# Attention and two MLP stages on one core: four like PSUM slots in place of two kinds of bank

## The chip, the cores and the metric

The kernel runs on one core of one Trainium2 chip. The metric is the device time of one execution in microseconds (us). Before the change its median is 464.29 us over three runs (463.94 to 465.4).

## What is computed

Causal attention over 2 batches of 12 heads (448 tokens, 64 wide), then two MLP stages on the 896 tokens of 768 values. All in float32.

```python
scores = (q @ k.T) / sqrt(64), causal mask
attn = exp(scores - max); attn = attn / (sum + 1e-9)
x = attn @ v                          # heads side by side: 896 x 768
h = x @ w_in                          # 896 x 1024
solu = h * softmax(h)
x = layernorm(solu) * g_ln @ w_out    # 896 x 768
out = relu(x @ w_in2) ** 2 @ w_out2   # 2048 wide in between
```

## The kernel before

The 24 heads are worked as 12 pairs; a pair's two heads lie on partitions 0 to 63 and 64 to 127. For each pair i the string `SEQ` (line 27) names these steps, and its order is the order of the instructions on every engine, written out by hand; each engine's queue is in order.

- `load_r`, `load_v` (SP queue) fetch keys with queries, and values. `H` (ACT, line 255) rounds keys and queries to float32r, `L` (DVE, line 259; pair 0 on POOL) takes the rest.
- `S0a`, `S0b`, `S0c` (PE, line 270) are rough scores of row blocks 3, 2 with 0, and 1. `mxa`, `mxb`, `mxc` (DVE, line 285) take the maximum of each row. `mT` (PE, line 293) transposes the eight columns of maxima, `row` (ACT, line 298) copies them out of PSUM, and `rowd` (SP, lines 310 and 314) writes them as rows of `MR`. Pair 0 goes another way (`mxr`, line 305).
- `Sa`, `Sb` (PE, lines 329, 337, 345) are the exact scores in two halves, the maximum subtracted by a matmul of `NEG1` with `MR`. `ea1`, `eb1` (ACT, line 361) are their exponentials, `ka`, `kb` (POOL, line 358) the mask.
- `Ua`, `Ub` (PE, line 370) multiply with the values. `EA`, `EB` (ACT, line 382) copy the result of either head out of PSUM. `sums`, `recips`, `rcd`, `spread`, `norm`, `x_hi`, `x_lo` divide by the row sums, by way of three transfers, and leave `xT`.
- `wf`, `wh`, `wl` prepare the weights of the first MLP. `h0.c` to `h6.c` (PE, line 488) are the six matmuls of one token tile with chunk c; the last attention steps are mixed with them. Then come `y` (line 635), the second MLP's `h` (line 769) and `o` (line 798).
- `fl` (line 517) is two matmuls of 448 columns whose result nobody reads: `NEG1` by the zeros in `MR[2]`. There are ten, all ahead of the first exact scores.

PSUM has eight banks of 512 float32 a partition. Before, `bank2` hands out two slots of two banks (exact scores, fills, `h`), and `bank` four single banks (each head's rough scores, each head's U, the transpose). A slot is taken from the head of a list and put back at its end when the step that reads it stands in the order; the wait on that reader is attached to the first instruction that writes the slot. When `EB` of the last pair has been placed, the four single banks become two more slots of two.

```python
bs = [bank("mxp") for h in range(2)]            # max_mm
UB[i] = [bank("U") for h in range(2)]           # pv
nc.scalar.activation(ee[i][:, h, :], U[:, 0:S], AF.Identity, bias=SE)   # EA, EB
nc.tensor.matmul(b[:, j % 2, 0:S], NEG1, MR[2][:, 0:S], start=True, stop=True)  # fl
```

Of the kernel before, what the change touches and what calls it, by code (L numbers as in the profile page):

```python
# [26 lines left out]
SEQ = """
load_r.0 lq.0 fl.0 fl.1 fl.2 H.0 load_r.1 fl.3 lq.8 lq.1 L.0 S0b.0 fl.4 mxb.0 fl.5 S0a.0 fl.6 mxa.0 S0c.0 H.1 load_r.2
fl.7 lq.4 fl.8 mxc.0 load_v.0 S0c.1 fl.9 mxc.1 S0a.1 mxr.0 lq.2 mxa.1 S0b.1 Sa.0 mxb.1 H.2 load_r.3 mT.1 S0a.2 row.1
Sb.0 ea1.0 mxa.2 load_v.1 ka.0 lq.3 lq.5 S0b.2 eb1.0 rowd.1 Ua.0 mxb.2 lq.9 H.3 kb.0 L.1 S0c.2 Ub.0 mxc.2 load_r.4 L.2  # L30
mT.2 Sa.1 row.2 L.3 EA.0 rowd.2 EB.0 S0a.3 ea1.1 Sb.1 lq.6 mxa.3 sums.0 lq.10 S0c.3 ka.1 eb1.1 mxc.3 load_r.5 S0b.3
load_v.2 mxb.3 Sa.2 H.4 kb.1 S0c.4 mT.3 mxc.4 Sb.2 row.3 L.4 rowd.3 S0b.4 Ua.1 recips.0 mxb.4 rcd.0 H.5 load_r.6 ea1.2
wf.0 Ub.1 eb1.2 spread.0 load_v.3 S0a.4 EA.1 Sa.3 EB.1 kb.2 mxa.4 sums.1 S0c.5 Sb.3 ka.2 mxc.5 mT.4 norm.0 S0b.5 row.4
wh.0 mxb.5 Ua.2 rowd.4 ea1.3 recips.1 rcd.1 x_hi.0 ka.3 S0a.5 load_v.4 H.6 Ub.2 mxa.5 eb1.3 wl.0 S0a.6 spread.1 EA.2
Sa.4 load_r.7 EB.2 kb.3 mxa.6 sums.2 mT.5 Sb.4 row.5 x_lo.0 ea1.4 rowd.5 L.5 S0b.6 Ua.3 norm.1 mxb.6 H.7 recips.2
S0c.6 Ub.3 rcd.2 mxc.6 ka.4 eb1.4 load_r.8 x_hi.1 L.6 S0a.7 EA.3 Sa.5 EB.3 kb.4 mxa.7 spread.2 lq.7 mT.6 Sb.5 row.6
L.7 sums.3 ea1.5 rowd.6 S0c.7 x_lo.1 Ua.4 H.8 load_v.5 ka.5 mxc.7 eb1.5 norm.2 S0b.7 recips.3 Ub.4 mxb.7 rcd.3
load_v.6 L.8 S0c.8 load_r.9 EA.4 Sa.6 EB.4 kb.5 mxc.8 spread.3 Sb.6 wf.1 lq.11 sums.4 mT.7 Ua.5 row.7 x_hi.2 rowd.7
ea1.6 H.9 load_r.10 S0b.8 x_lo.2 Ub.5 mxb.8 eb1.6 norm.3 wh.1 recips.4 S0a.8 rcd.4 mxa.8 Sa.7 load_v.7 ka.6 EA.5 EB.5
S0c.9 kb.6 mT.8 mxc.9 Sb.7 sums.5 row.8 x_hi.3 spread.4 wl.1 ea1.7 S0a.9 rowd.8 Ua.6 eb1.7 mxa.9 load_r.11 ka.7 H.10  # L40
x_lo.3 S0b.9 recips.5 Ub.6 norm.4 mxb.9 rcd.5 S0a.10 Sa.8 mxa.10 kb.7 EA.6 spread.5 x_hi.4 mT.9 L.9 S0c.10 EB.6 Sb.8
row.9 sums.6 ea1.8 x_lo.4 Ua.7 rowd.9 mxc.10 H.11 L.10 load_v.8 eb1.8 ld.3 norm.5 S0b.10 recips.6 Ub.7 rcd.6 mxb.10
S0b.11 kb.8 x_hi.5 Sa.9 mxb.11 EA.7 ka.8 EB.7 mT.10 Sb.9 wf.2 sums.7 row.10 ea1.9 rowd.10 S0a.11 Ua.8 eb1.9 spread.6
load_v.9 ka.9 mxa.11 wh.2 Sa.10 recips.7 x_lo.5 rcd.7 S0c.11 Sb.10 mxc.11 norm.6 mT.11 load_v.10 Ub.8 row.11 ea1.10
rowd.11 L.11 x_hi.6 spread.7 Ua.9 EA.8 x_lo.6 eb1.10 kb.9 EB.8 ka.10 Sa.11 sums.8 load_g.0 kb.10 Ub.9 ld.4 norm.7
recips.8 Sb.11 wf.3 Ua.10 EA.9 ea1.11 EB.9 x_hi.7 h0.0 sums.9 eb1.11 load_v.11 wl.2 rcd.8 h0.1 wh.3 kb.11 h1.0 wf.4
spread.8 Ub.10 ld.5 h0.2 wl.3 wh.4 h1.1 recips.9 ka.11 rcd.9 x_lo.7 Ua.11 norm.8 Ub.11 wf.5 EA.10 x_hi.8 h1.2 EB.10
sums.10 h0.3 spread.9 wl.4 wh.5 h1.3 x_lo.8 wl.5 h0.4 norm.9 recips.10 h0.5 rcd.10 h1.4 mx.0 EA.11 h1.5 spread.10
EB.11 ex.0 sums.11 h2.0 x_hi.9 x_lo.9 h2.1 de.0 norm.10 recips.11 mx.1 rcd.11 h2.2 mu.0 h2.3 x_hi.10 spread.11 sq.0
x_lo.10 h3.0 ex.1 va.0 pw.0 h2.4 mu.1 norm.11 h2.5 sq.1 h3.1 mx.2 x_hi.11 h3.2 de.1 ex.2 x_lo.11 va.1 lw.0 h3.3 pw.1  # L50
mu.2 h3.4 fa.1 fa.0 de.2 ln.0 h3.5 sq.2 T.0 mx.3 lw.1 h4.0 va.2 ex.3 of.0 pw.2 h4.1 ln.1 h4.2 Th.0 fa.2 mu.3 oh.0 h4.3
ln.2 lw.2 ol.0 T.1 sq.3 of.1 h4.4 h4.5 de.3 oh.1 Tl.0 h5.0 Th.1 lw.3 mx.4 h5.1 va.3 ex.4 Tl.1 h6.0 pw.3 mu.4 T.2 l2.0
h5.2 de.4 sq.4 fa.3 ol.1 lw.4 h5.3 ln.3 of.2 h5.4 Th.2 T.3 of.3 h5.5 h6.1 mx.5 lw.5 h6.2 Tl.2 ex.5 h6.3 Th.3 de.5 mu.5
h6.4 oh.3 Tl.3 sq.5 h6.5 lw.6 va.4 oh.2 y0.0 mx.6 ol.2 ex.6 ol.3 y0.1 de.6 va.5 mu.6 lw.7 pw.5 l2.1 pw.4 l2.2 fa.4
of.4 ln.4 y0.2 fa.5 oh.4 of.5 y0.3 sq.6 ol.4 oh.5 va.6 ln.5 T.4 ol.5 pw.6 y0.4 Th.4 of.6 Tl.4 oh.6 y0.5 fa.6 ol.6 ln.6
of.7 T.5 y0.6 Th.5 oh.7 Tl.5 ol.7 T.6 y0.7 Th.6 Tl.6 f2.0 y1.0 yo.1 g2.0 f2.1 o2.0 y1.1 yp.0 yo.2 g2.1 yo.0 o2.1 y1.2
yp.1 yp.2
# [3 lines left out]
def attention_moe_kernel(tc, kq, v, w_in, w_out, g_ln, w_in2, w_out2, out):  # L61
# [27 lines left out]
    def f(ap):  # L89
        return ap.bitcast(F32)  # L90

    with es:
# [84 lines left out]
        with att:  # L177
# [6 lines left out]
            pv_ = ExitStack()
            ps_t = [pv_.enter_context(pool(f"pt{j}", space=PSUM)) for j in range(4)]

            def bank(nm):

                pl = ps_t.pop(0)
                t = pl.tile([P, 512], F32, tag="t", name=nm)  # L190
                slot_of[id(t)] = (pl, t)
                return t
# [662 lines left out]
```

## Time and profile before

| | |
|---|---|
| three runs, median (lowest to highest) | 464.29 us (463.94 to 465.4) |
| the profiled execution, its own time | 464.8 us |
| its span, first to last instruction | 463.1 us |
| PE busy | 454.7 us, 98% of the span |
| DVE, ACT, POOL busy | 273.4, 165.7, 121.6 us |

PE is TensorE's matmuls, PEld its weight loads, DVE VectorE, ACT ScalarE, POOL GpSimd, SP the queue that issues all the transfers here. A span of an engine says when its instructions ran; what ended the idle time before one stands behind an arrow. The ends of matmuls are modelled, so distances between starts are the safer measure on PE.

### The profile page before, as it was taken

Reading aid. Unit: us, or ns where it says so; the run is one execution under the profiler, and the core shown is the slowest. Engines: PE = TensorE matmul, PEld = TensorE weight load, DVE = VectorE, ACT = ScalarE, POOL = GpSimd, SP = SyncE. Lnnn points to the kernel's source line nnn. Section 1 sums busy time; section 2 is a strip of 40 time slices with the busy share of each in tenths; the row PEclk is TensorE's granted clock in tenths of the full one; section 3 lists DMA queues with packets and bytes.
Section 4 is the critical chain, followed back from the end, with each engine's and each line's share of the span. In section 5 each row is a group of like instructions: output and inputs, shape, how many; then the busy total and the mean of one; then the engine's idle time right before and its main releaser. Section 6 shows DMA issues by size and latency. Waiting matters only on the chain.

```text
span 463.1 us, 6653 instructions
## 1 busy us (share of the span) xinstructions
PE 454.7 (98%) x2537; PEld 403.4 (87%) x2537; DVE 273.4 (59%) x523; ACT 165.7 (36%) x225; POOL 121.6 (26%) x122
## 2 busy tenths in 40 slices
...
PEclk9999999999999999999999999999999999999999
...
GB/s 256 171 153 123 118 173 101 151 136 132 37 162 115 206 265 9 0 1 0 0 82 124 124 81 137 75 130 107 98 136 70 137 85 120 219 106 137 79 59 119
DMA packets 42416, 52.48 MB, mean 113 GB/s; under 512 B 18960, under 2 KB 33040, under 8 KB 42000
## 3 DMA queue, kind: packets, MB, share of 16 engines
...
HBM read 49.16 MB, written 2.80 MB: 112 GB/s over the span
## 4 chain that ended last, share of the span: by engine, by line
PE 86%; DVE 2%; POOL 1%; ACT 1%; issue 1%; DMA 1%; SPq 1%; ACTq 0%; DVEq 0%; POOLq 0%
PE h L769 25%; PE o L798 25%; PE y L635 13%; PE h L488 12%; PE U L370 6%; PE s L329 2%; PE T L613 1%; PE mxp L270 1%; POOL x L412 1%; DMA bc<-d 1%; DVE JK L285 1%; PE s L337 1%; ACT E L382 0%; PE mT L293 0%; SPq L310 0%
## 5 line engine op out<-in xcount | busy, mean ns | idle before, releaser
L769 PE MATMUL h<-yT,w 128*128 128x448 f32 x576 | 116.9, 365 | 0.0
L798 PE MATMUL o<-w,g 128*128 128x384 f32 x672 | 116.7, 336 | 0.0
L798 PEld LDWEIGHTS o<-w,g 128*128 128x128 f32 x672 | 116.5, 188 | 0.0
L769 PEld LDWEIGHTS h<-yT,w 128*128 128x128 f32 x576 | 108.2, 188 | 8.6
L691 POOL TENSOR_TENSOR w<-wf,w 128x768 fp32r<-128x768 f32 x32 | 59.3, 1854 | 209.5 <-ACT w L688 209.5
L150 DVE TENSOR_SCALAR wf<-raw 128x768 int32<-128x768 int32 (+1 forms) x46 | 26.4, 574 | 88.0 <-DMA raw<-in_moe_w_out_dram 57.7
L688 ACT CAST w<-wf 128x768 fp32r<-128x768 f32 x32 | 26.8, 838 | 137.4 <-DVE wf L152 113.2
L488 PE MATMUL h<-w,xT 128*128 128x512 f32 x252 | 59.3, 393 | 0.6 <-ACT PP L361 0.6
L635 PE MATMUL y<-lnT,w 128*128 128x384 f32 (+1 forms) x288 | 58.9, 365 | 0.0
L635 PEld LDWEIGHTS y<-lnT,w 128*128 128x128 f32 x288 | 51.9, 188 | 5.9
L488 PEld LDWEIGHTS h<-w,xT 128*128 128x128 f32 x252 | 46.8, 188 | 10.4 <-ACT PP L361 0.7
L151 DVE SCALAR_TENSOR_TENSOR wf<-raw,wf 128x768 int32<-128x768 int32 (+1 forms) x46 | 48.1, 1046 | 1.6
L370 PE MATMUL U<-PP,VR 128*128 128x448 f32 (+1 forms) x192 | 48.8, 400 | 0.0
L285 DVE CUSTOM_DVE_ANT_0 JK<-mxp,MK 112x336 bf16<-112x336 f32 (+2 forms) x96 | 40.1, 447 | 13.6 <-PE mxp L270 10.0
L152 DVE SCALAR_TENSOR_TENSOR wf<-raw,wf 128x768 int32<-128x768 int32 (+1 forms) x46 | 45.8, 995 | 1.6
L370 PEld LDWEIGHTS U<-PP,VR 128*128 128x128 f32 x192 | 32.0, 190 | 15.2 <-issue 9.6
L412 POOL TENSOR_TENSOR x<-E,bc 64x448 f32<-64x448 f32 x24 | 28.2, 1176 | 32.6 <-DMA bc<-d 19.2
L358 POOL TENSOR_SCALAR_AFFINE_SELECT PP<-PP 128x256 f32<-128x256 f32 (+1 forms) x48 | 25.3, 558 | 34.9 <-ACT PP L361 34.3
L755 DVE TENSOR_TENSOR relu<-h,relu 128x896 f32<-128x896 f32 x16 | 17.5, 1092 | 14.6 <-ACT relu L754 14.6
L361 ACT ACTIVATE PP<-s 128x1024 f32<-128x1024 f32 x24 | 24.2, 1016 | 1.6 <-PE s L345 1.2
L757 ACT CAST g<-relu 128x896 fp32r<-128x896 f32 x16 | 15.1, 942 | 18.6 <-DVE relu L755 18.6
L382 ACT ACTIVATE E<-U,SE 128x448 f32<-128x448 f32 x24 | 14.4, 633 | 19.1 <-POOL x L412 19.0
...
## 6 DMA issues: line engine op xcount, KB each, us to landing
...
```

Of the source, the lines that this page charges most:

```text
L150: nc.vector.tensor_scalar(xi, hw, 3, 0x3FFFFFFF, ALU.logical_shift_left, ALU.bitwise_and)
L151: nc.vector.scalar_tensor_tensor(xi, hw, -0x40000000, xi, ALU.bitwise_and, ALU.bitwise_or)
L152: nc.vector.scalar_tensor_tensor(xi, lw, 29, xi, ALU.logical_shift_right, ALU.bitwise_or)
L285: nc.vector.tensor_tensor_reduce(JK[t], bs[h][0:JP, o : o + nk], MK[:, S - nk :], 1.0, NEG, ALU.add, ALU.max, mx[i][:, 4 * h + t : 4 * h + ...
L370: nc.tensor.matmul(UB[i][h][:, q0:S], VR[i % 3][:, t, h, :], PP[(2 * i + a) % NPP][:, h, o : o + nq], start=t == 0, stop=t == 2,)
L412: nc.gpsimd.tensor_tensor(x[D * h : D * h + D], e[0:D, h], bc[:, h], ALU.mult)
L488: nc.tensor.matmul(b[:, half, :], xT[c][s][:, t * P : t * P + P], W1[c][:, w, 512 * half : 512 * half + 512], start=(c == 0 and s == 0 and ...
L635: nc.tensor.matmul(b[:, ci, 0:n], WO[fi][:, w, c * P : c * P + P], M["lnT"][a][s][:, fi, :], start=(fi == 0 and w == 0 and s == 0), stop=( ...
L688: nc.scalar.copy(W2[n][:, 0], w_f["2", n])
L691: nc.gpsimd.tensor_tensor(W2[n][:, 1], w_f["2", n], f(W2[n][:, 0]), ALU.subtract)
L769: nc.tensor.matmul(b[:, a, 0:HT], W2[fi][:, w, c * P : c * P + P], yT[c][s][:, HT * a : HT * a + HT], start=(c == 0 and w == 0 and s == 0) ...
L798: nc.tensor.matmul(ob, G[fi + e][s][:, P * t : P * t + P], w, start=(fi + e == 0 and r == 0), stop=(fi + e == NF2 - 1 and r == 2),)
```

## The change

Four slots of two banks serve everything from the start: rough scores of both heads in one slot, U of both heads in one slot. The maxima of pairs 1 to 11 are transposed into a free corner (columns 400 to 511) of the slot that held `S0c`, which is given back only after `row`. `EA` and `EB` become one `E` over both heads. `rowd` issues two transfers for both heads where there were four. The fills read a tile `Z` of 128x128 zeros, set first on DVE, its first column broadcast; there are nine, not ten. `SEQ` is written anew throughout (its lines are left out here).

```diff
-        add_slots(2)
+        add_slots(4)
...
+            Z = qk.tile([P, P], F32R, name="Z")
...
+            nc.vector.memset(f(Z), 0.0)
             nc.vector.memset(f(NEG1), 0.0)
-            nc.vector.memset(f(MR[2]), 0.0)
...
-                bs = [bank("mxp") for h in range(2)]
+                b = bank2("mxp")
...
-                    give1(bs[h])
+                if g == "c" and i:
+                    st["c", i] = b
+                else:
+                    give(b)
...
-                T = bank("mT")
-                nc.tensor.transpose(T[0:8, 0:JP], mx.pop(i), ident[:JP, :JP])
-                return T
+                b = st.pop(("c", i))
+                nc.tensor.transpose(b[0:8, 0, 512 - JP :], mx.pop(i), ident[:JP, :JP])
+                return b
...
-                for h in range(2):
-                    nc.sync.dma_start(
-                        f(MR[i % 3][D * h : D * h + 1, D:]).rearrange("o (t p) -> o t p", p=JP),
-                        f(m2[4 * h : 4 * h + 4]),
-                    )
-                    nc.sync.dma_start(f(MR[i % 3][D * h : D * h + 1, 0:D]), f(m2[4 * h + 3 : 4 * h + 4, JP - D :]))
+                rows = f(MR[i % 3])[0:P:D]
+                nc.sync.dma_start(rows[:, D:].rearrange("h (t p) -> h t p", p=JP), f(m2))
+                nc.sync.dma_start(rows[:, 0:D], f(m2[3:8:4, JP - D :]))
...
-                    UB[i] = [bank("U") for h in range(2)]
+                    UB[i] = bank2("U")
...
-            def u_out(n, U):
-                i, h = divmod(n, 2)
-                if h == 0:
-                    ee[i] = lat.tile([P, 2, S], F32, tag="E", name="E", bufs=2)
-                nc.scalar.activation(ee[i][:, h, :], U[:, 0:S], AF.Identity, bias=SE)
-                give1(U)
+            def u_out(i):
+                U = UB.pop(i)
+                ee[i] = lat.tile([P, 2, S], F32, tag="E", name="E", bufs=2)
+                nc.scalar.activation(ee[i], U[:, :, 0:S], AF.Identity, bias=SE)
+                give(U)
...
-                    nc.tensor.matmul(b[:, j % 2, 0:S], NEG1, MR[2][:, 0:S], start=True, stop=True)
+                    nc.tensor.matmul(b[:, j % 2, 0:S], Z, Z[:, 0:1].broadcast_to((P, S)), start=True, stop=True)
```

How the order changes is shown at three places. PE at the start of the program, before the change (HI_124 is pair 0, HI_125 pair 1; 336 and 112 columns are `S0b`, 448 `S0a`, 224 `S0c`):

```order
L517 MATMUL fill<-MR_132,NEG_133 128x448 x8
L270 MATMUL mxp<-HI_124 128x336 x2
L270 MATMUL mxp<-HI_124 128x112 x2
L517 MATMUL fill<-MR_132,NEG_133 128x448 x4
L270 MATMUL mxp<-HI_124 128x448 x2
L517 MATMUL fill<-MR_132,NEG_133 128x448 x2
L270 MATMUL mxp<-HI_124 128x224 x2
L517 MATMUL fill<-MR_132,NEG_133 128x448 x4
L270 MATMUL mxp<-HI_125 128x224 x2
L517 MATMUL fill<-MR_132,NEG_133 128x448 x2
L270 MATMUL mxp<-HI_125 128x448 x2
```

The same place after it (HI_118 is pair 0, HI_119 pair 1):

```order
L503 MATMUL fill<-Z 128x448 x10
L257 MATMUL mxp<-HI_118 128x336 x2
L257 MATMUL mxp<-HI_118 128x112 x2
L257 MATMUL mxp<-HI_118 128x224 x2
L503 MATMUL fill<-Z 128x448 x2
L257 MATMUL mxp<-HI_118 128x448 x2
L503 MATMUL fill<-Z 128x448 x4
L257 MATMUL mxp<-HI_119 128x448 x2
L257 MATMUL mxp<-HI_119 128x224 x2
L503 MATMUL fill<-Z 128x448 x2
L257 MATMUL mxp<-HI_119 128x336 x2
```

Two more fill matmuls stand ahead of the first rough scores, and `S0c` of pair 0 follows on `S0b` with no fill between.

The SP queue at its first maxima rows (`MR` from `m`), before:

```order
L221 DMA r<-in_kq_dram 128x896
L224 DMA VR_141<-in_v_dram 128x8x64
L472 DMA raw<-in_moe_w_in_dram 128x512 x2
L310 DMA MR_131<-m_302 1x4x112
L314 DMA MR_131<-m_302 1x16x4
L310 DMA MR_131<-m_302 1x4x112
L314 DMA MR_131<-m_302 1x16x4
```

and after:

```order
L208 DMA r<-in_kq_dram 128x896
L211 DMA VR_136<-in_v_dram 128x8x64
L301 DMA MR_125<-m_311 2x4x112
L302 DMA MR_125<-m_311 2x64
L458 DMA raw<-in_moe_w_in_dram 128x512
L208 DMA r<-in_kq_dram 128x896
```

The maxima of a pair take two issues in place of four. Ahead of this place the queue now fetches the keys of pairs 0, 1 and 2 and the values of pair 0 before any weights; before, four blocks of weights stood between them.

PE where the attention passes into the first MLP, before (PP_143 is the first half of pair 10, 126 and 129 pair 11):

```order
L329 MATMUL s<-LO_129,HI_126 128x192 x2
L337 MATMUL s<-MR_132,NEG_133 128x320 x2
L337 MATMUL s<-MR_132,NEG_133 128x192 x2
L370 MATMUL U<-PP_143,VR_141 128x448
L370 MATMUL U<-PP_143,VR_141 128x64
L370 MATMUL U<-PP_143,VR_141 128x448
L370 MATMUL U<-PP_143,VR_141 128x64
L488 MATMUL h<-w,xT_71 128x512 x4
```

and after (120 and 123 are pair 11):

```order
L317 MATMUL s<-LO_123,HI_120 128x320 x2
L317 MATMUL s<-LO_123,HI_120 128x192 x2
L325 MATMUL s<-MR_126,NEG_127 128x320 x2
L325 MATMUL s<-MR_126,NEG_127 128x192 x2
L474 MATMUL h<-w,xT_71 128x512 x4
L474 MATMUL h<-w,xT_72 128x512 x2
```

The first `h` now stands ahead of both U halves of pair 10: eight pieces of `h`, of three token tiles, come before `Ua.10`, where none did.

## Rows read from the trace of the kernel before

**Rows 1.** The page: the span, and busy time by engine with the granted clock.
```profile
span 463.1 us, 6653 instructions
...
PE 454.7 (98%) x2537; PEld 403.4 (87%) x2537; DVE 273.4 (59%) x523; ACT 165.7 (36%) x225; POOL 121.6 (26%) x122
...
PEclk9999999999999999999999999999999999999999
```
**Rows 2.** Windows: from:to, length, busy us by engine, granted clock, DMA share, GB/s.
```profile
2.20:10.87 8.67, 8.67 (x31) 5.91 (x31) 6.92 (x28) 2.29 (x4) 2.38 (x2) 1.00 0.98 300
10.87:99.15 88.28, 85.55 (x640) 63.61 (x639) 67.68 (x217) 49.44 (x74) 39.20 (x60) 1.00 0.54 146
99.15:459.64 360.49, 360.47 (x1868) 333.84 (x1868) 197.69 (x274) 112.17 (x147) 78.47 (x51) 1.00 0.32 101
459.64:463.10 3.46, 0.00 (x0) 0.00 (x0) 0.05 (x1) 0.48 (x1) 0.00 (x0) 1.00 0.48 171
```
**Rows 3.** Waits of PE, whole span: us in total, times, longest.
```profile
PE fill L517 <- DVE NEG L232: 2.2, 1, 2.2
PE s L329 <- ACT PP L361: 0.6, 1, 0.6
PE h L488 <- ACT PP L361: 0.6, 1, 0.6
PE mxp L270 <- DVE mx L285: 0.4, 2, 0.2
PE mT L293 <- DVE mx L285: 0.4, 1, 0.4
PE mT L293 <- ACT E L382: 0.2, 1, 0.2
PE mxp L270 <- ACT E L382: 0.2, 1, 0.2
```
**Rows 4.** Timeline of PE at the start: start us, length, what.
```profile
2.20 3.35 PE L517 MATMUL fill<-MR,NEG 128*128 128x448 f32 x8 [2.20 <-DVE NEG L232]
5.48 0.74 PE L270 MATMUL mxp<-HI 64*128 64x336 f32 x4
...
8.96 1.07 PE L517 MATMUL fill<-MR,NEG 128*128 128x448 f32 x4
9.96 0.37 PE L270 MATMUL mxp<-HI 64*128 64x224 f32 x2
...
14.26 0.26 PE L293 MATMUL mT<-ident,mx 112*8 112x112 f32 x1
```
**Rows 5.** Timeline of DVE and ACT at the start.
```profile
0.88 0.17 DVE L227 MEMSET NEG<- 128x128 f32 x1 [0.88 <-PEq L842]
...
6.39 0.51 DVE L285 CUSTOM_DVE_ANT_0 JK<-mxp,MK 112x336 bf16<-112x336 f32 x1 [0.58 <-PE mxp L270]
...
8.16 0.62 DVE L285 CUSTOM_DVE_ANT_0 JK<-mxp,MK 112x448 bf16<-112x448 f32 x1 [0.40 <-PE mxp L270]
...
10.57 0.39 DVE L285 CUSTOM_DVE_ANT_0 JK<-mxp,MK 112x224 bf16<-112x224 f32 x1
...
12.75 0.50 DVE L285 CUSTOM_DVE_ANT_0 JK<-mxp,MK 112x336 bf16<-112x336 f32 x1
...
13.40 0.51 DVE L285 CUSTOM_DVE_ANT_0 JK<-mxp,MK 112x336 bf16<-112x336 f32 x1
...
14.03 0.08 DVE L285 DVE_READ_ACCUMULATOR2_ANT mx<- 112x1 f32 x1
...
4.04 0.94 ACT L255 CAST HI<-r 128x896 fp32r<-128x896 f32 x1 [1.98 <-DMA r<-in_kq_dram]
```
**Rows 6.** The chain that ended last, 42.39 to 49.90 (ten pieces): start, length, what.
```profile
42.39 0.85 PE s L329 x12
...
49.50 0.40 PE mxp L270 x2
```
**Rows 7.** ACT: the two copies of U, and one activation of 896 columns from PSUM.
```profile
34.40 1.16 ACT L382 ACTIVATE E<-U,SE 128x448 f32<-128x448 f32 x2
...
L754 ACT ACTIVATE relu<-h 128x896 f32<-128x896 f32 x16 | 14.6, 912 | 1.4 <-PE h L769 1.4
```
**Rows 8.** Issues of the maxima rows on SP: ns min/median/max, first and last start.
```profile
L310 SPq DMA_DIRECT2D MR<-m x22: 620/638/758, 14.8 to 90.1; - x22
L314 SPq DMA_DIRECT2D MR<-m x22: 508/526/602, 15.6 to 90.7; - x22
```

More of the change, by code (lines that the diff above doesn't have):

```diff
@@ L24 @@
 XLO_POOL = ()
-ATT = ("recips", "rcd", "spread", "norm", "x_hi", "x_lo", "EA", "EB", "Ua", "Ub", "sums")
+ATT = ("recips", "rcd", "spread", "norm", "x_hi", "x_lo", "E", "Ua", "Ub", "sums")
 SEQ = """
-load_r.0 lq.0 fl.0 fl.1 fl.2 H.0 load_r.1 fl.3 lq.8 lq.1 L.0 S0b.0 fl.4 mxb.0 fl.5 S0a.0 fl.6 mxa.0 S0c.0 H.1 load_r.2
-fl.7 lq.4 fl.8 mxc.0 load_v.0 S0c.1 fl.9 mxc.1 S0a.1 mxr.0 lq.2 mxa.1 S0b.1 Sa.0 mxb.1 H.2 load_r.3 mT.1 S0a.2 row.1
-Sb.0 ea1.0 mxa.2 load_v.1 ka.0 lq.3 lq.5 S0b.2 eb1.0 rowd.1 Ua.0 mxb.2 lq.9 H.3 kb.0 L.1 S0c.2 Ub.0 mxc.2 load_r.4 L.2
@@ L31 @@
[L31 to L50, printed above, removed]
@@ L56 @@
-of.7 T.5 y0.6 Th.5 oh.7 Tl.5 ol.7 T.6 y0.7 Th.6 Tl.6 f2.0 y1.0 yo.1 g2.0 f2.1 o2.0 y1.1 yp.0 yo.2 g2.1 yo.0 o2.1 y1.2
-yp.1 yp.2
+load_r.0 fl.0 fl.1 fl.2 fl.3 H.0 load_r.1 fl.4 L.0 S0b.0 S0c.0 mxb.0 fl.5 S0a.0 fl.6 mxc.0 fl.7 mxa.0 H.1 load_r.2
+load_v.0 lq.4 S0a.1 mxr.0 S0c.1 lq.0 fl.8 mxc.1 S0b.1 Sa.0 mxa.1 mxb.1 H.2 load_r.3 L.1 ea1.0 load_v.1 mT.1 S0b.2 Sb.0
+row.1 mxb.2 ka.0 rowd.1 L.2 lq.1 S0a.2 S0c.2 Ua.0 mxa.2 H.3 load_r.4 eb1.0 mxc.2 S0a.3 kb.0 mT.2 mxa.3 Sa.1 row.2 lq.2
+rowd.2 L.3 S0c.3 Ub.0 ea1.1 load_r.5 mxc.3 ka.1 S0b.3 E.0 Sb.1 mxb.3 sums.0 Sa.2 H.4 eb1.1 mT.3 L.4 Sb.2 load_r.6
@@ new lines @@
+row.3 lq.3 ea1.2 kb.1 recips.0 S0b.4 rowd.3 Ua.1 mxb.4 H.5 rcd.0 eb1.2 L.5 lq.8 S0c.4 lq.5 S0a.5 S0a.4 kb.2 mxc.4
+load_v.2 Ub.1 mxa.4 ka.2 spread.0 mT.4 E.1 Sa.3 wf.0 row.4 sums.1 Sb.3 ea1.3 rowd.4 S0b.5 H.6 Ua.2 load_v.3 norm.0
+mxa.5 eb1.3 load_r.7 wh.0 recips.1 S0c.5 mxb.5 Ub.2 rcd.1 ld.3 kb.3 mxc.5 E.2 wl.0 mT.5 Sa.4 row.5 sums.2 x_hi.0 L.6
+rowd.5 ea1.4 S0a.6 Sb.4 ka.3 mxa.6 lq.6 S0c.6 spread.1 ka.4 eb1.4 S0b.6 mxc.6 Ua.3 load_r.8 mxb.6 H.7 kb.4 S0b.7
+x_lo.0 mT.6 lq.7 Sa.5 L.7 row.6 load_v.4 rowd.6 norm.1 recips.2 S0a.7 ea1.5 mxb.7 Ub.3 rcd.2 load_r.9 mxa.7 S0c.7 Sb.5
@@ new lines @@
+ka.5 x_hi.1 mxc.7 load_v.5 Sa.6 x_lo.1 eb1.5 spread.2 wf.1 E.3 mT.7 Sb.6 ea1.6 sums.3 Ua.4 lq.9 row.7 load_r.10 H.8
+norm.2 S0b.8 eb1.6 recips.3 S0a.8 mxb.8 Ub.4 rcd.3 wh.1 rowd.7 kb.5 mxa.8 S0c.8 load_v.6 E.4 Ua.5 mxc.8 ka.6 spread.3
+x_hi.2 sums.4 H.9 L.8 mT.8 Sa.7 row.8 x_lo.2 load_r.11 L.9 rowd.8 Sb.7 ea1.7 norm.3 recips.4 S0b.9 rcd.4 H.10 S0a.9
+Ub.5 load_v.7 mxa.9 eb1.7 lq.10 mxb.9 kb.6 x_hi.3 S0c.9 Sa.8 spread.4 E.5 mxc.9 kb.7 S0a.10 sums.5 ea1.8 mT.9 mxa.10
+Sb.8 ka.7 row.9 lq.11 S0c.10 rowd.9 Ua.6 x_lo.3 L.10 norm.4 recips.5 S0b.10 rcd.5 eb1.8 Ub.6 mxb.10 load_v.8 load_g.0
```

50 lines of the change are left out of this document (24 added, 26 removed).

## The prediction

> **What bounds the kernel now.** First the page's busy line [rows 1]: PE works 454.7 of 463.1 us, so at most 8.4 us of the span are without it, and the granted clock reads full (the 2.4 GHz level) throughout. Then the windows, cut where PE's work changes [rows 2]. From 99.15 to 459.64 PE is busy 360.47 of 360.49 us: nothing waits there, and the last 3.46 us are the copy and the store of the last tile. From 10.87 to 99.15, the attention pairs, PE lacks 88.28 - 85.55 = 2.73 us. Up to 2.20 it waits for a memset, and from there to 10.87 it is busy, but mostly with fills. So a change that leaves PE's useful work as it is can win only ahead of 99.15: by a faster start, or by taking away the 2.73 us. Everything behind moves along, because PE runs it without a gap.
>
> The waits of PE [rows 3] name who ends last: exponentials that give back a slot (0.6 and 0.6), maxima on DVE (0.4 and 0.4), copies of U (0.2 and 0.2). Each is 0.2 to 0.65 us. PE's work for one pair is the stretch of the chain from 42.39 to 49.90 [rows 6], ten pieces with nothing between them: 7.51 us. DVE needs for a pair's maxima 14.03 - 10.57 = 3.5 us [rows 5], and over the whole stretch is busy 67.68 of 88.28 us; ACT 49.44, POOL 39.20 [rows 2]. No other engine is full, but DVE is close enough that its order matters.
>
> **The start.** Fills wait for DVE's memsets up to 2.20 [rows 4]. The first memset ends at 0.88 + 0.17 = 1.05 [rows 5]; `Z` now stands there, so the fills can begin near 1.11, 1.09 us earlier. The first eight lie 3.28 us apart from start to start of what follows (2.20 to 5.48), 0.41 each [rows 4]. Ten of them end at 1.11 + 4.1 = 5.21. Pair 0's keys are rounded by 4.04 + 0.94 = 4.98 [rows 5], and since their load is still the first in the queue I take that as it is. So `S0b.0` starts at 5.21 and not at 5.48, 0.27 earlier, and DVE's first maximum with it (6.39 to 6.12). From here DVE sets the pace: maxima of pairs 0 and 1 back to back up to 14.03 + 0.08, after which the transpose follows at 14.26 [rows 4, 5]. DVE waited once in between, 0.40 us ahead of 8.16, for a matmul behind four fills; now `S0c.0` follows `S0b.0` without fills, so DVE has work. Together 0.27 + 0.40 = **0.67 us** off the start. Bounds: 1.09 us if DVE could follow all of it; nothing if a load is later than before. A later load I think unlikely, since the keys of pairs 1 and 2 now go ahead of weights. One fill pair less (0.5 to 0.8 us of PE, four take 9.96 - 8.96 = 1.0 us further on, 0.25 each [rows 4]) is worth nothing by itself, as PE waits for DVE at the transpose anyway. What a matmul on a broadcast column costs no row shows; between 0.25 and 0.41 each I take it like the old fill, with the same cover.
>
> **The pairs.** Here I walked the new order by hand: PE's pieces with the lengths of the chain's pieces, DVE's groups with those of rows 5, each slot taken from the list in order and free when its reader is done. The waits of before go: the copies of U are one instruction, near 0.91 us by one of 896 columns from PSUM, against 1.16 for two [rows 7], 0.25 us less of ACT a pair; the transpose takes no slot; exact scores choose from four slots, not two. In the walk PE meets a slot that is not free only by tenths, at the transposes of pairs 2 and 4 (DVE's last group of the pair ends 0.1 late) and at `S0b.1`. At some nine further places the reader is done less than 0.4 us ahead, DVE most often. My walk knows no transfer that lands late and no small gap, so I leave four waits of 0.2 us, the usual size in rows 3: 0.8 us. Saved: 2.73 - 0.8 = **1.9 us**. The bounds are 2.73 (no wait left) and nothing (waits as long, elsewhere).
>
> **What costs nothing, and its cover.** Two issues less a pair for the maxima rows, 0.64 + 0.53 = 1.17 us of SP [rows 8]: PE never waits for `MR` in rows 3, and now the rows are there sooner. If the merged transfers landed later, the exact scores would wait, and exponentials, U and the whole pair with them; they move the same bytes, so I price it at zero. SP's other loads are moved with the list, each by places ahead of a use that lies several us later in the walk. The single-bank pools' early closing is gone; `h` now finds a slot as soon as the exponentials of pair 10 are done, and the 0.6 us ahead of the first `h` [rows 3] (part of the 2.73) goes. The later stages have the same matmuls and four slots in both; their 360 us have cover of their own and stay.
>
> **Sum.** 0.67 + 1.9 = 2.6 us. Against the profiled execution's 464.8 us that makes 462.2. It stands 0.5 us over the median of the three runs, 464.29, against which I predict **461.7 us**. What a measurement of this kernel tells from no change is about 0.3%, 1.4 us.
>
> A rule weighed against this: the Trainium skill, PSUM — Partial Sum Buffer, section on bank collisions, asks that engines be kept apart bank by bank, not address by address. By that rule the old single banks were rightly free as soon as one head's half was read, and the new slots are kept longer than the chip needs. The trace shows the half: the second head's reading starts 0.65 us after the first's. The sum would lose that only where PE stands waiting; the price is the second rival's.
>
> **Rivals.**
> 1. *The waits only move.* DVE's load is the same, and slots are shared by more users: the 2.73 us come back at other readers, and only the start is won: 464.29 - 0.67 = 463.6 us. For it: DVE is busy 77% of the stretch, and the nine close places. Against: two causes of the old waits (the half copies, two slots for exact scores) are gone as such. 25%, together with a start that wins nothing (464.3).
> 2. *Slots come back later, and it is slower.* A slot of rough scores is free only when both heads' maxima are taken; the first head's bank used to be free about half a group sooner, 13.40 - 12.75 = 0.65 us for group b [rows 5]. `S0c`'s slot is held until `row` on top. If PE arrives in that half group once a pair, 11 pairs lose 11 x 0.65 = 7.2 us: 464.29 - 0.67 - 2.73 + 7.2 = 468.1 us. It beats the gain of 3.4 us from six pairs on, and shows as slower than before by over 1.4 us from eight on. Against it: my walk has PE come later than that at nearly all pairs, and U, 4 us of PE a pair, stands between most takings of a slot. 9%.
> 3. *No wait is left and the start is won in full:* 464.29 - 2.73 - 1.09 = 460.5 us. It needs DVE never to be late; it counts with the forecast, 66% together.
>
> **How the numbers follow.** Forecast 461.7. Low end: the third case less the 0.35 us by which the lowest run lies under the median, 460.2. High end: rival 1 without its start plus half a microsecond, the distance of the profiled run, 464.8. Left out are the second rival and the edges, under 2 in 10. Faster than by 1.4 us (under 462.9): 66%; within: 25%; slower: 9%.
>
> **What would show it.** Right: the fills start near 1.1 us; the first transpose near 13.6; the first `h` near 94 to 95 us, with `Ua.10` behind it (before 99.15, with 2.1 us of `Ua.10` ahead); PE's idle time in the pairs under 1 us; PE without a gap from the first `h` to the end. E 12 times near 0.91 us. Wrong: PE waiting for DVE's maxima or `row` at more than a few places; `Sa` or `Sb` waiting for a transfer into `MR`; or a wait behind the first `h`, for the last pairs' `x`, whose U halves now come after more of `h`.

## The result, and the profile after

| | before | after |
|---|---|---|
| median of four runs on the same chip | 464.69 us (463.94 to 465.4) | 460.65 us (460.07 to 461.63) |
| the profiled execution, its own time | 464.8 us | 461.63 us |
| its span | 463.1 us | 459.8 us |
| PE busy | 454.7 us | 452.7 us |

The time is 0.9915 of that before, with a 95% interval of 0.9898 to 0.9932: 3.9 us less. The forecast was 461.7 us. One profiled execution below, that of the new start in the kernel before, took 472.67 us where the median of its runs is 463.5, and its result is read from the times.

The same page lines and views as [rows 1, 2], of the kernel after. First the span and busy time by engine; the granted clock reads full in all 40 slices, as before.

```profile
span 459.8 us, 6525 instructions
...
PE 452.7 (98%) x2535; PEld 402.0 (87%) x2535; DVE 275.1 (60%) x524; ACT 164.6 (36%) x213; POOL 120.8 (26%) x122
```

To set the two traces against each other they are cut at the same events: the first transpose (`mT.1`), the first `h`, the end of PE's work. Windows of the kernel before; after length come busy us of PE, PEld, DVE, ACT, POOL with their counts, then granted clock, DMA share and GB/s:

```profile
14.26:99.15 84.89, 82.31 (x611) 60.87 (x611) 64.72 (x201) 48.81 (x73) 39.20 (x60) 1.00 0.52 138
```

and of the kernel after:

```profile
12.59:93.60 81.01, 79.37 (x603) 58.82 (x604) 66.43 (x202) 47.90 (x63) 34.20 (x54) 1.00 0.58 158
93.60:456.30 362.70, 362.57 (x1878) 335.07 (x1876) 197.82 (x273) 111.74 (x146) 82.64 (x57) 1.00 0.32 100
```

The start is shorter by 14.26 - 12.59 = 1.67 us. The pairs' window of before holds the eight matmuls of `Ua.10` that now stand behind the first `h`; they took 99.15 - 0.60 - 96.39 = 2.16 us there (the timeline below). Without them the pairs went from 84.89 - 2.16 = 82.73 to 81.01 us, 1.72 less. Of that, 0.94 us are idle time of PE (84.89 - 82.31 = 2.58 before, 81.01 - 79.37 = 1.64 after) and 0.78 us busy time (82.31 - 2.16 = 80.15 and 79.37), at 603 matmuls in both. With them moved, the later stages went from 360.49 + 2.16 = 362.65 to 362.70, and the tail from 3.46 to 3.50. The sum is -1.67 - 1.72 + 0.05 + 0.04 = -3.30 us, which is the difference of the spans (459.8 and 463.1). So the whole gain lies ahead of the first `h`, half of it in the first 14 us.

PE ahead of the first `h`, before:

```profile
96.39 2.16 PE L370 MATMUL U<-PP,VR 128*128 128x448 f32 x8
99.15 2.14 PE L488 MATMUL h<-w,xT 128*128 128x512 f32 x8 [0.60 <-ACT PP L361]
```

The waits of PE after, which answer to [rows 3]:

```profile
PE s L317 <- ACT PP L349: 1.5, 1, 1.5
PE fill L503 <- DVE Z L214: 1.1, 1, 1.1
PE mxp L284 <- DVE mx L272: 0.4, 1, 0.4
PE fill L503 <- DVE mx L272: 0.3, 1, 0.3
```

The old list of small waits in the pairs is gone, and a single one of 1.5 us stands in their place. The chain of waits says where it is from (start, length, what):

```profile
40.06 0.55 SPq L301
...
41.21 0.39 SPq L458
...
41.72 6.12 DMA bc<-d
...
47.98 1.16 POOL x L399
...
50.85 1.03 ACT PP L349
...
51.92 1.02 PE s L317 x10
```

The reciprocals of pair 1's sums are broadcast over 64 rows (`bc` from `d`); the transfer took 6.12 us to land, POOL's `norm` came late with it, `x_hi.1` on ACT waited for POOL, and `eb1.5`, which gives PE its slot, stood behind `x_hi.1` in ACT's queue. The transfer itself was issued behind the two transfers of maxima (the first is the row at 40.06) and a block of weights (41.21). This picture, a transfer behind others on SP that ends as a wait of PE for ACT, comes back in the experiments.

The start, which answers to [rows 4, 5]: PE, then DVE.

```profile
1.10 4.10 PE L503 MATMUL fill<-Z 128*128 128x448 f32 x10 [1.10 <-DVE Z L214]
...
12.59 0.26 PE L284 MATMUL mxp<-ident,mx 112*8 112x112 f32 x1 [0.43 <-DVE mx L272]
```

```profile
6.04 0.51 DVE L272 CUSTOM_DVE_ANT_0 JK<-mxp,MK 112x336 bf16<-112x336 f32 x1
...
8.58 0.08 DVE L272 DVE_READ_ACCUMULATOR2_ANT mx<- 112x1 f32 x1
8.70 0.62 DVE L272 CUSTOM_DVE_ANT_0 JK<-mxp,MK 112x448 bf16<-112x448 f32 x1
...
12.45 0.08 DVE L272 DVE_READ_ACCUMULATOR2_ANT mx<- 112x1 f32 x1
```

The first maximum starts at 6.04 and the last reading of pair 1 at 12.45, 6.41 us later; before it was 14.03 - 6.39 = 7.64 us [rows 5]. The same rows before, at the step from one head to the next:

```profile
8.71 0.08 DVE L285 DVE_READ_ACCUMULATOR2_ANT mx<- 112x1 f32 x1
8.94 0.62 DVE L285 CUSTOM_DVE_ANT_0 JK<-mxp,MK 112x448 bf16<-112x448 f32 x1
```

From the start of the reading to the start of the next head went 0.23 us, and now 0.12. The maxima themselves have not become shorter. `E` is one instruction of 1.01 us:

```profile
31.14 1.01 ACT L369 ACTIVATE E<-U,SE 128x896 f32<-128x896 f32 x1 [3.11 <-PE U L358]
```

### The profile page after: what moved, and what is told of

It is laid out like the page before. It is cut to its first block, busy times and chain, and to the rows that moved or that the text cites. A ratio compares the mean times of both kernels' runs of the same rounds, so it can differ in the third digit from the quotient of the medians.

```text
span 459.8 us, 6525 instructions
## 1 busy us (share of the span) xinstructions
PE 452.7 (98%) x2535; PEld 402.0 (87%) x2535; DVE 275.1 (60%) x524; ACT 164.6 (36%) x213; POOL 120.8 (26%) x122
## 4 chain that ended last, share of the span: by engine, by line
PE 93%; DMA 1%; POOL 1%; ACT 0%; issue 0%; SPq 0%; ACTq 0%; POOLq 0%
PE h L752 25%; PE o L781 25%; PE y L621 13%; PE h L474 13%; PE U L358 9%; PE s L317 4%; PE mxp L257 1%; DMA bc<-d 1%; PE T L599 1%; PE s L325 1%; POOL x L399 1%; PE mxp L284 0%; PE s L333 0%; ACT PP L349 0%; SPq L301 0%
## 5 line engine op out<-in xcount | busy, mean ns | idle before, releaser
L399 POOL TENSOR_TENSOR x<-E,bc 64x448 f32<-64x448 f32 x24 | 31.9, 1328 | 47.2 <-DMA bc<-d 42.7
L272 DVE CUSTOM_DVE_ANT_0 JK<-mxp,MK 112x336 bf16<-112x336 f32 (+2 forms) x96 | 38.8, 446 | 8.5 <-PE mxp L257 7.5
L346 POOL TENSOR_SCALAR_AFFINE_SELECT PP<-PP 128x256 f32<-128x256 f32 (+1 forms) x48 | 19.7, 443 | 21.3 <-ACT PP L349 20.8
L650 DVE TENSOR_TENSOR yT<-y,yT 128x384 fp32r<-128x384 f32 (+1 forms) x12 | 7.4, 624 | 22.7 <-ACT yT L649 22.7
```

The source lines that it names most:

```text
L272: nc.vector.tensor_tensor_reduce(JK[t], b[0:JP, h, o : o + nk], MK[:, S - nk :], 1.0, NEG, ALU.add, ALU.max, mx[i][:, 4 * h + t : 4 * h + ...
L399: nc.gpsimd.tensor_tensor(x[D * h : D * h + D], e[0:D, h], bc[:, h], ALU.mult)
```

## The experiments

Each was run beside the kernel before on the same chip (464.6 to 464.9 us, on three chips in all), and a ratio below is to that. The theory A behind them: two things win, a shorter start and waits that went with the new slots and their order. Its rivals B name one other cause each.

### The new slots in the old order

The kernel after, with the string `SEQ` of before. `EA` and `EB` become `E` where `EB` stood, and three steps move by a place or two (the `SEQ` of before, and of this kernel, `E` left aside), so that none asks for a slot that only a later one gives back.

```diff
-rowd.3 S0b.4 Ua.1 recips.0 mxb.4 rcd.0 H.5
+rowd.3 S0b.4 recips.0 mxb.4 Ua.1 rcd.0 H.5
...
-mT.4 norm.0 S0b.5 row.4
+mT.4 norm.0 row.4 S0b.5
...
-mT.7 Ua.5 row.7
+mT.7 row.7 Ua.5
```

> The change's code (four slots, one E, two transfers, fills from Z) with the order of before; three takings of a slot (Ua.1, S0b.5, Ua.5) stand one releasing step later, since the order of before asks for a fifth slot there; PE's own order is that of before. Theory A (the start is won by the code, the pairs by the order that fits the slots): first transpose about 13.0 us (before 14.26, after 12.59), PE's waits from there to the first h still 2.5 us or more, span 461.5 to 462.3. Rival B (the slots by themselves take the waits away, whatever the order): waits under 1.5 us and span under 461.

Measured: 470.12 us (467.17 to 476.47), ratio 1.0083 (1.0054 to 1.0112). The waits of 2.5 us or more came, as theory A had it, but the span is 471.9 us, far over what either theory had. The start is not won either: the fills begin at 1.10, but PE then waits 0.47 us for pair 0's keys, at 4.93, and the first transpose comes at 14.38, where about 13.0 was expected. One of PE's two longest waits in the pairs, 1.6 us each:

```profile
PE U L358 <- DVE mx L272: 1.6, 1, 1.6
```

It is `Ua.1`, which in this order can take a slot only behind the last maxima that give one back. It costs more than itself, as the timeline of PE and the windows there show (granted clock third from the end):

```profile
30.11 7.05 PE L358 MATMUL U<-PP,VR 128*128 128x448 f32 x16 [1.58 <-DVE mx L272]
...
43.00 3.78 PE L358 MATMUL U<-PP,VR 128*128 128x448 f32 x8 [1.63 <-DVE sr L380]
```

```profile
30.00:32.00 2.00, 1.89 (x4) 1.10 (x5) 1.93 (x3) 1.95 (x3) 0.00 (x0) 0.50 0.73 236
...
34.00:36.00 2.00, 2.00 (x6) 1.61 (x6) 0.00 (x0) 0.00 (x0) 1.71 (x3) 0.50 0.35 57
```

After the wait the granted clock stands at 0.50, the 1.2 GHz level, from 30 to 36 us, and behind the other, of 1.63 us, again from 44 to 46. Two executions took 467.2 us at a mean granted clock of 0.996, and three 470.0 to 473.6 us at 0.989. Like slots in the old order are therefore slower; the order before wants a fifth slot at three places. The run mixes that with the moved steps and with the clock, so what the slots do by themselves it does not tell.

### The kernel before, heads taken in the other order

PE writes head 0's bank, then head 1's. Taking the maxima of head 1 first leaves DVE no new matmul to wait for at head 0.

```diff
-                for h in range(2):
+                for h in (1, 0):
```

> The kernel before, only that DVE takes the second head's maxima first, so that one wait for PE covers both heads. Theory A (a second semaphore in a wait makes the step between the two heads 0.1 us longer, three times a pair; that is where 0.7 us of the start went): the step from the end of one head's reading to the start of the other's falls from 0.22 to 0.12 us, first transpose at 13.5 to 13.7 instead of 14.26, time 0.5 to 1.0 us under before. Rival B (the longer step comes from reading another bank or from the accumulator read, not from the wait): step stays at 0.22, time within 0.3 us of before.

Measured: 464.38 us, ratio 0.9992 (0.9983 to 1.0001). DVE at the same place as above:

```profile
7.99 0.08 DVE L285 DVE_READ_ACCUMULATOR2_ANT mx<- 112x1 f32 x1
8.11 0.62 DVE L285 CUSTOM_DVE_ANT_0 JK<-mxp,MK 112x448 bf16<-112x448 f32 x1
```

The step is 0.12 us, as after the change, so a second wait on a matmul cost about 0.11 us a step. The first transpose came at 13.37, 0.89 us earlier (some of it because PE's fills also reached their quicker pace earlier here). But the first `h` came at 98.51, only 0.64 earlier, and the time moved by 0.4 us, where 0.5 to 1.0 was expected: a quicker DVE alone finds other waits in the old pairs (`Sa` or `Sb` for an exponential 1.0, before 0.6), and the profiled execution lost 0.7 us more at `o`. The mechanism is confirmed, its worth alone is at the edge of what is measured.

### The old fills in the new kernel

```diff
-            nc.vector.memset(f(Z), 0.0)
             nc.vector.memset(f(NEG1), 0.0)
+            nc.vector.memset(f(MR[2]), 0.0)
...
-                    nc.tensor.matmul(b[:, j % 2, 0:S], Z, Z[:, 0:1].broadcast_to((P, S)), start=True, stop=True)
+                    nc.tensor.matmul(b[:, j % 2, 0:S], NEG1, MR[2][:, 0:S], start=True, stop=True)
```

> The change with the fills of before (NEG1 by the zeros of MR[2], their memsets first). The fills begin at 2.2 instead of 1.1 us. Theory A (fills stand ahead of the first rough scores and DVE follows at once): first rough scores near 6.2 instead of 5.13, first transpose near 13.6 instead of 12.59, time 0.8 to 1.1 us over the change. Rival B (the start is set by DVE's memsets up to 5.94 and by the loads): first transpose within 0.3 us of 12.59, time within 0.3 us of the change.

Measured: 461.51 us, ratio 0.9931 (0.9918 to 0.9944), 0.9 us over the change's 460.65. The timeline of PE:

```profile
2.20 4.10 PE L502 MATMUL fill<-MR,NEG 128*128 128x448 f32 x10 [2.20 <-DVE NEG L218]
...
13.69 0.26 PE L283 MATMUL mxp<-ident,mx 112*8 112x112 f32 x1 [0.28 <-DVE mx L271]
```

Fills, first rough scores and first transpose are all 1.10 us later than after the change, and so is the span (460.9 against 459.8; both executions have the wait for ACT, 1.7 and 1.5 us). Ten fills on a broadcast column took 4.10 us, and ten on the old tile 4.10 us. So the early `Z` is worth 1.1 us of the start, once ten fills stand ahead of the scores as the new order has them.

### The new kernel without its one wait

`x_hi.1` and `x_lo.1` behind `eb1.5`:

```diff
-ka.5 x_hi.1 mxc.7 load_v.5 Sa.6 x_lo.1 eb1.5 spread.2
+ka.5 mxc.7 load_v.5 Sa.6 eb1.5 x_hi.1 x_lo.1 spread.2
```

> The change with x_hi.1 and x_lo.1 moved one step back, behind eb1.5. Theory A (PE's 1.52 us wait at 51.92 comes from ACT's queue: x_hi.1 waits there for the normalisation, whose broadcast landed 6.1 us after its issue, and eb1.5 stands behind it): the wait falls under 0.3 us, time 1.0 to 1.4 us under the change. Rival B (the release is late for another reason, or the wait comes back at the next step, E.3 or row.7): PE's waits in the pairs stay over 1.2 us, time within 0.3 us of the change.

Measured: 459.9 us (459.65 to 460.36), ratio 0.9896 (0.9883 to 0.991), span 457.8. The wait is gone: all of PE's waits (for the fills' zeros 1.1, for a slot of the fills 0.7, for the first transpose 0.4, for the first keys 0.3) lie in the start. It looked like a gain of 0.7 us. The last experiment takes all of it back: the change itself measures 459.77 us there. In this profile the broadcast also came early (POOL starts `norm.1` at 46.12, after the change at 47.98), so whether the edit by itself takes the wait away is not shown.

### The old order of the weights' loads in the new kernel

```diff
-load_r.0 fl.0 fl.1 fl.2 fl.3 H.0 load_r.1 fl.4
+load_r.0 lq.0 fl.0 fl.1 fl.2 fl.3 H.0 load_r.1 lq.8 lq.1 fl.4
```

(`lq.2` and `lq.4` are put back the same way; the later places of these five are struck.)

> The change with the first transfers in the order of before: the weight parts lq.0, lq.8, lq.1, lq.4, lq.2 between the first keys and values. Theory A (the start was won by fills and DVE; loads only had to be no later): pair 1's keys rounded near 7.8 instead of 5.1 us, its S0a.1 and S0c.1 then near 8.9, which is about when DVE needs them (9.25): first transpose 12.6 to 12.9, time within 0.5 us of the change. Rival B (the load order carried the larger part of the start): first transpose 13.3 or later, time 0.8 us or more over the change.

Measured: 459.88 us, ratio 0.9896 (0.9882 to 0.991). The first transpose stayed at 12.59. Against the 459.77 us of the change in the last experiment, it shows no gain from keys that go ahead of weights.

### Four transfers of the maxima in the new kernel

```diff
-                rows = f(MR[i % 3])[0:P:D]
-                nc.sync.dma_start(rows[:, D:].rearrange("h (t p) -> h t p", p=JP), f(m2))
-                nc.sync.dma_start(rows[:, 0:D], f(m2[3:8:4, JP - D :]))
+                for h in range(2):
+                    nc.sync.dma_start(
+                        f(MR[i % 3][D * h : D * h + 1, D:]).rearrange("o (t p) -> o t p", p=JP),
+                        f(m2[4 * h : 4 * h + 4]),
+                    )
+                    nc.sync.dma_start(f(MR[i % 3][D * h : D * h + 1, 0:D]), f(m2[4 * h + 3 : 4 * h + 4, JP - D :]))
```

> The change with the four transfers a pair for the maxima rows as before. Theory A (these rows are there long ahead of the exact scores): no wait of PE for a transfer, time within 0.5 us of the change. Rival B (1.1 us more of SP a pair delays the sums and broadcasts behind them, on which ACT's x_hi and PE's 1.5 us wait hang): that wait grows by 0.5 to 1.2 us and the time with it.

Measured: 465.92 us (463.35 to 470.44), ratio 1.0023 (0.9998 to 1.0048): over 5 us slower than the change, which the prediction had at nothing. PE's waits:

```profile
PE s L328 <- DMA MR<-m: 1.7, 2, 1.0
...
PE U L361 <- DMA VR<-in_v_dram: 1.1, 1, 1.1
```

Exact scores wait for `MR`, twice, and U for its values. The chain shows the queue ahead of the second of them:

```profile
46.51 0.66 SPq L301
...
47.88 0.62 SPq L301
...
48.55 4.22 DMA MR<-m
```

Head 1's row is issued 1.37 us behind head 0's and lands 4.22 us after that, at 52.77; the wait ends at 52.91. Then, as in the first experiment, the clock (PE's timeline, and a window; between the two rows shown lies one more wait for `MR`, 0.67 us at 52.91):

```profile
51.78 0.46 PE L328 MATMUL s<-MR,NEG 64*128 64x512 f32 x1 [1.04 <-DMA MR<-m]
...
56.04 3.97 PE L361 MATMUL U<-PP,VR 128*128 128x448 f32 x8
```

```profile
53.00:59.00 6.00, 6.00 (x24) 3.92 (x25) 2.82 (x4) 2.72 (x4) 2.24 (x2) 0.50 0.71 194
```

Eight matmuls of U took 3.97 us where the same eight took 2.16 before. Neither theory had it so: the waits are those of transfers in SP's queue, and the clock adds to them. Of the excess in the profiled span, 464.5 - 459.8 = 4.7 us, the waits are 1.7 + 1.1 = 2.8, while the change's 1.5 is not there; six microseconds at 0.50 cost up to 3.0. The fall is not the whole of it: two executions at a granted clock of 1.00 took 463.35 and 463.84 us, 3 to 4 us over the change.

### `E` in two again

```diff
-                nc.scalar.activation(ee[i], U[:, :, 0:S], AF.Identity, bias=SE)
+                for h in range(2):
+                    nc.scalar.activation(ee[i][:, h, :], U[:, h, 0:S], AF.Identity, bias=SE)
```

> The change with the copy of U as two activations, one a head, out of the same slot. Theory A (ACT is off the path apart from the one wait): 1.16 instead of 1.01 us of ACT a pair, time within 0.4 us of the change. Rival B (the later release of U's slot is met by PE): a new wait of PE for E, time 0.5 us or more over the change.

Measured: 460.18 us, ratio 0.9904 (0.989 to 0.9918). That is 0.4 us over the 459.77 of the change in the last experiment, on another chip, and the intervals overlap: copying both heads at once wins nothing that these runs can tell.

### Values' ones set on POOL, with `x_hi.1` later

```diff
-                nc.vector.memset(VR[i][:, :, :, D:], 1.0)
+                nc.gpsimd.memset(VR[i][:, :, :, D:], 1.0)
```

(and the edit of `SEQ` of the new kernel without its wait)

> The change with x_hi.1 and x_lo.1 one step later, and the ones of VR set by POOL instead of DVE (1.56 us of DVE ahead of its first maximum). Theory A (DVE's memsets hold the first maximum, 5.86 to 6.04, where the rough scores are ready near 5.6): first maximum 5.6 to 5.8, first transpose 12.1 to 12.3, time 0.1 to 0.3 us under the change with x_hi.1 later alone. Rival B (the matmul's end sets it): no difference.

Measured: 459.93 us, ratio 0.9897 (0.9883 to 0.9911). DVE's first maximum now waits for its matmul and starts at 6.06, where it was 6.04 with the memsets in front in the profile after. At that pace of PE the memsets are not what sets it. In the profiles of the kernel without its one wait and of the change once more PE's rough scores are sooner done, and DVE starts at 5.86, straight behind the memsets; there they can hold it, and the times show no gain from moving them.

### Two transfers of the maxima in the kernel before

The merge of `rowd` alone, the same edit as in the change.

> The kernel before with the two merged transfers a pair alone. Theory A (the merge is worth only what the order needs: the order of before leaves room for four issues, and PE never waits there for a maxima row): time within 0.5 us of before. Rival B (SP is short of time in any order): 1.0 us or more faster.

Measured: 462.6 us, ratio 0.9962 (0.9948 to 0.9976): 1.8 us less, from the one edit that was priced at nothing. PE's waits behind the fills:

```profile
PE mxp L270 <- DVE mx L285: 0.4, 2, 0.2
PE mT L293 <- DVE mx L285: 0.4, 1, 0.4
```

Against [rows 3], all four lines that end in ACT are gone, 0.6 + 0.6 + 0.2 + 0.2 us, and the two that end in DVE are left as they were. The window of the pairs:

```profile
14.34:97.08 82.74, 81.71 (x611) 60.80 (x611) 64.60 (x201) 49.15 (x73) 40.12 (x60) 1.00 0.51 140
```

The pairs take 82.74 us where they took 84.89, with the same matmuls, slots and order, and the time from the first `h` to the end of PE's work stays (360.62 and 360.49 us). Cut at the transposes, 1.30 of the 2.15 us lie between those of pairs 3 and 4 (27.02 to 36.92 before, 27.11 to 35.71 here), 0.23 between those of pairs 4 and 8, and 0.63 from there to the first `h`.

How SP reaches PE by way of ACT is not the same at each wait. The largest is at 33.64. SP, ACT and PE there, of the kernel before:

```profile
26.50 0.37 SPq L221 DMA_DIRECT2D r<-in_kq_dram  x1
```

```profile
31.73 0.94 ACT L255 CAST HI<-r 128x896 fp32r<-128x896 f32 x1 [4.13 <-PE U L370]
```

```profile
33.64 0.50 PE L329 MATMUL s<-HI 64*128 64x448 f32 x4 [0.65 <-ACT PP L361]
```

and with two transfers, where PE does not wait:

```profile
25.08 0.38 SPq L221 DMA_DIRECT2D r<-in_kq_dram  x1
```

```profile
30.51 0.94 ACT L255 CAST HI<-r 128x896 fp32r<-128x896 f32 x1 [2.82 <-DMA r<-in_kq_dram]
```

ACT rounds the keys of pair 5 here (`H.5`), and the exponentials that give PE its slot stand behind that in its queue. The load of these keys stands on SP behind the maxima rows of pair 2, four issues before and two now. It is issued 1.42 us sooner, and the rounding starts 1.22 us sooner, while PE is 0.09 us later. In the kernel before the trace names a matmul of U as the end of ACT's idle time; that the keys were what it waited for is taken from the second trace, which names their transfer. The wait of 0.16 us at 35.61 is for the copies of U behind the same exponentials.

The wait of 0.60 us ahead of the first `h` takes another way. The chain, of the kernel before:

```profile
88.68 0.68 SPq L310
...
91.35 3.26 DMA bc<-d
...
94.75 1.15 POOL x L412
...
98.08 1.02 ACT PP L361
```

Behind the four issues for pair 11 goes the broadcast of the reciprocals of pair 7; POOL's `norm` waits for it, ACT's copy for the tile that `norm` reads, and the exponential stands behind the copy. With two transfers the broadcast is issued 2.54 us behind the last transpose, where it was 3.28. The wait of 0.18 us at 66.38 goes back by a copy and a `norm` to DVE in the chain, and not to a transfer; why it is gone too is open.

POOL's and ACT's waits summed over the span do not show this. POOL's for the broadcast fell from 19.2 to 10.4 us and ACT's for POOL from 19.0 to 11.2, but in the profile of the next experiment they are 7.4 and 11.7 us with PE's waits for ACT all there, and in the profile after POOL waits 42.7 us for the broadcast.

### The new start in the kernel before

`Z` for the fills and the heads swapped, all else as before.

```diff
+            nc.vector.memset(f(Z), 0.0)
...
-                for h in range(2):
+                for h in (1, 0):
...
-                    nc.tensor.matmul(b[:, j % 2, 0:S], NEG1, MR[2][:, 0:S], start=True, stop=True)
+                    nc.tensor.matmul(b[:, j % 2, 0:S], Z, Z[:, 0:1].broadcast_to((P, S)), start=True, stop=True)
```

> The kernel before with the fills from Z and the second head's maxima read first: only the start of the change, everything else as before. Theory A (the start is fills plus DVE's shorter steps, 1.67 us at the first transpose): first transpose 12.5 to 13.0 us instead of 14.26, time 0.8 to 1.6 us under before, PE's waits in the pairs still 2 us or more. Rival B (the later waits eat the start): first transpose as early, time within 0.5 us of before.

Measured: 463.5 us, ratio 0.9982 (0.9963 to 1.0). Some 0.8 us, half of what the start of the changed kernel wins, and the interval reaches 1. In the profiled execution PE's waits for ACT in the pairs are still there (1.1, 0.7 and 0.2 us).

### Both small edits of the new kernel together

The old order of the loads and `x_hi.1` behind `eb1.5`.

> The change with x_hi.1 and x_lo.1 one step later and the first transfers in the order of before. Theory A (the 1.5 us wait was a late broadcast, which either edit takes away): no wait of PE over 0.4 us behind the first transpose, time as with either edit alone, 4.6 to 5.1 us under before. Rival B (the edits add up): another 0.5 us or more.

Measured: 459.9 us, ratio 0.9899 (0.9884 to 0.9915): they do not add.

### The change once more

The kernel after, without an edit.

> The change itself once more, beside the others on one chip. Theory A (the 1.5 us wait for the exponential hangs on when a broadcast lands, and comes in some executions only): its times spread over 1 us or more, between 459.9 and 461.6. Rival B (it comes in all): all executions within 0.4 us of 461.2.

Measured: 459.77 us (459.57 to 460.05, five runs), ratio 0.9897 (0.9882 to 0.9912). Its profiled execution does not have the wait of 1.5 us, and its span is 457.8 us. POOL at `norm.1` here, and in the profile after:

```profile
46.19 2.35 POOL L399 TENSOR_TENSOR x<-E,bc 64x448 f32<-64x448 f32 x2 [3.62 <-DMA bc<-d]
```

```profile
47.98 2.36 POOL L399 TENSOR_TENSOR x<-E,bc 64x448 f32<-64x448 f32 x2 [5.18 <-DMA bc<-d]
```

By the same program POOL starts 1.8 us later in the one than in the other. The broadcast was issued at 41.48 here and at 41.72 there, so 1.55 us of it lie between issue and start. The five times do not spread over 1 us, as theory A had it, nor do they lie at 461.2, as B had it; but of two profiles of one program one has the wait of 1.5 us and one has not, and the variants that seemed to take it away (459.88 to 459.93 us) are no faster than the change is here.

## Why the prediction was right, and where not

**The time and its place.** 460.65 us lies in the range, 1.05 under the forecast (the second measurement, 459.77, lies under the low end of 460.2), and the gain is ahead of the first `h`, as the prediction argued from PE's window without a gap: the later stages differ by 0.05 us. The fills start at 1.10 (forecast 1.11), the first rough scores at 5.13 (5.21), the first `h` at 93.60 (94 to 95), and no wait appears behind it.

**The start: right in kind, too small.** The term was 0.67 us, with 1.09 as its bound; it measured 1.67. Read from the rows: the first maximum is 6.39 - 6.04 = 0.35 us earlier (forecast 0.27). The span from there to the last reading is 7.64 - 6.41 = 1.23 us shorter, of which the wait ahead of 8.16 and the step it stands in are 0.49 (forecast 0.40). The rest was not in the sum: the steps from head to head, 0.23 to 0.12 at four places and about 0.035 to nothing at two, 0.5 us together, and a gap of 0.23 between pairs 0 and 1. The transpose follows its last reading by 0.14 instead of 0.23, which is the last 0.09. Part of the 0.35 and the 0.49 may be PE's pace: the fills behind the first rough scores lie 0.38 us apart before and 0.33 after, and no run separates that. The step that failed is "maxima of pairs 0 and 1 back to back": the durations were taken and the distances between them were not, though [rows 5] give 14.03 - 10.57 = 3.5 us for a pair and the maxima in it are shorter than that. That the bound of 1.09 was passed has this cause: it counted the fills alone. The swapped heads show the step's mechanism, the old fills in the new kernel the 1.1 us of `Z`.

**The pairs: near in size, in part by luck; wrong in cause.** 1.9 us was forecast, all of it as waits, and 1.72 measured. Only 0.94 of that is idle time: 1.64 us of waits are left where four of 0.2 were allowed, 1.5 of it in one, and the sign "under 1 us" was missed in this profile (in the second measurement 0.13 us are left). The other 0.78 is busy time, which the sum took as fixed. The kernel before with two transfers has the same, 0.60 us less busy time at the same 611 matmuls, so a wait seems to cost more than the idle time in front of it. That is a reading of two traces, and no run tests it. The reasons given for the 1.9, the single `E` and the choice among four slots, are not what the runs show. `E` takes 1.01 us, where 0.91 was forecast, and in two again it costs nothing measurable. New slots in the old order lost 5 us, with the moved steps and the clock in it; what the choice among four wins by itself no run shows. The kernel before gains 1.8 us, and its pairs 84.89 - 82.74 = 2.15, by the merge of two transfers alone. The failed step is "PE never waits for `MR` in rows 3", from which the two issues were priced at zero. The sentence is true of the kernel before, yet three of the four waits for ACT in the same rows (0.65, 0.60 and 0.16 us) hung on SP's queue: two on a load of keys and one on a broadcast, each behind four small issues. That the merge is not free in the other direction either, four transfers in the new order show: there the exact scores do wait for `MR`, and over 5 us are lost, the fall of the clock included. Tracing back what made each exponential of [rows 3] late, at 33.64 to the load issued at 26.50 and at 99.15 to the broadcast issued at 91.35, would have found it before.

**How the parts add.** By itself the merge gives 1.8 us and the new start 0.8; the change gives 3.9, and 4.8 in its second measurement. What is left, 1.3 to 2.2 us, falls to the new order with its slots together. Two things can make it up: ten fills ahead of the scores, so that `Z` is used in full (1.1 us by the old fills in the new kernel), and an order in which a quicker DVE meets no old wait. The second is argued from the traces, and no run shows its share. What like slots would win alone stays open: the old order asks for more of them than there are, and the new order could not be run on the old slots, which lack a bank at some of its steps.

**The rivals.** The second, slots that come back half a group later, did not come true in the change's order: the one PE wait for a slot of maxima is the fills' 0.3 us at the start. By the Trainium skill, PSUM — Partial Sum Buffer, section on bank collisions, engines are to be kept apart by bank, so single banks could be handed back sooner; the trace has nothing to say against the rule, it shows only that in this order nobody stood waiting for the half. In the old order PE did stand waiting for a slot that maxima give back, at `Ua.1`, with 1.58 us and a clock at 0.50 behind it, which the rival's price had left out. The third, no wait left and a full start, is what the second measurement of the change shows: 459.77 us, and 79.45 us of pairs with 79.32 busy; the 460.5 worked out for it was 0.7 us high. In that profile both terms pass their bounds: the first transpose comes at 12.35, 1.91 us earlier (1.09 at most), and the pairs are 82.73 - 79.45 = 3.28 us shorter (2.73 at most). The window from the first transpose to the first `h` there:

```profile
12.35:91.80 79.45, 79.32 (x604) 58.83 (x604) 65.77 (x202) 47.82 (x63) 34.76 (x54) 1.00 0.56 161
```
